# Scores and state sums of a retention layer as 64x64 quarters of TensorE, with the order of all steps rewritten

## The chip, the cores and the metric

One NeuronCore of a Trainium2 chip runs the whole program. The metric is the device time of one execution in microseconds (us); the kernel before takes 430.01 us (median of three runs, 429.88 to 433.79). All times in this document are of that kind or come from one profiled execution of the kernel.

## The reference

A chunked linear-attention ("retention") layer is followed by a gated feed-forward layer. Cut to what matters:

```python
# q, k, v: (4 batches, 8 heads, 768 positions, 64); block = 64
for b in range(12):
    intra = (qb @ kb.T * Dmask) @ vb              # inside the block
    inter = (qb * lam_pow) @ kv_state             # from all earlier blocks
    out[b] = intra + inter
    kv_state = lam ** 64 * kv_state + (kb * rev_pow).T @ vb
x_prev = x shifted by one position                # x: heads side by side, 512 wide
xk = mu_k * x + (1 - mu_k) * x_prev;  xr = mu_r * x + (1 - mu_r) * x_prev
out = sigmoid(xr @ w_r) * (relu(xk @ w_k) ** 2 @ w_v)     # 512 -> 1024 -> 512
```

## The kernel before

**Tiling.** The 768 positions are worked on as NT = 6 blocks n of 128 positions, each of two 64-position halves (eo = 0 and 1). The eight heads are four pairs hp; the two heads of a pair (ab = 0 and 1) fill the 128 partitions. For each (n, hp) there are these steps, named by one letter, and the small letters name what VectorE (DVE), ScalarE (ACT) or GpSimd (POOL) do:

- `L` and `N` (`load_hp`, `load_qv`): DMAs on SyncE's queue (SP) that bring keys, then queries and values, into one of two buffers `in` (hp 0 and 2 share one, `in_104`; hp 1 and 3 the other, `in_105`). Block 0 comes as one DMA of four parts.
- `M` (`clear`): two memsets on POOL that put zeros beside queries and values, so that a 128-row product of one head of the pair has zeros where the other head's rows would be.
- `A` (`scores`): in blocks 1 to 5, eight fp32 matmuls, each with 128 rows (both heads), 64 output columns of the array and 128 moving columns; half of the moving operand is zeros. Result in the PSUM tile `sc`. `a` (`decay`) multiplies it by the decay mask into the SBUF tile `mv` on DVE, and `q` (`decay_queries`) puts the scaled queries beside it (four DVE instructions).
- `U` (`sums`): eight fp32 matmuls of the same shape, keys against values with zeros, into the PSUM tile `u`: the state's increments of both halves. Block 5 needs only the first half and already used 64x64. `u` and `w` (`even_state`, `odd_state`) update the state on DVE and copy it beside the values on ACT.
- `B` (`values`): sixteen fp32 matmuls of 128 rows, 64 array columns and 64 moving columns, into the PSUM tile `xp`.
- `e E f F` mix the result with its shifted copy (ACT, POOL, DVE); `y x` split it into a high and a low part (ACT, DVE).

In block 0, `A`, `U` and `B` use other shapes. Then come the dense products of the feed-forward layer, each fp32 product made of three fp32r passes (high x high, high x low, low x high) of 128x128 by 512 columns: `R` and `Q` (`rp`), `K` (`kp`, with `h` and `p` on ACT and DVE after them), `V` (`vp`, with `o` multiplying by the gate and sending the output). Block 0 runs `R` and `K` as plain fp32. At the start the weights are loaded (`S`) and brought from their int64 transport form into fp32 parts (`c` on ACT and POOL, `C` on DVE, `D` on ACT and DVE).

**Order.** A string `ORDER` lists every step, such as `A21` (scores, block 2, pair 1). A loop emits them in that order, and the class `InOrder` keeps every engine's instructions in the order of emission, so that an engine whose next instruction waits does nothing else. There is no other scheduler. Because the helper class records every operation, all instructions have line L30 in the profile.

**PSUM.** Of eight banks, `sc` has two buffers of one bank, `u` and `xp` one each, and the dense products share four.

Of the kernel before, what the change touches and what calls it, by code (L numbers as in the profile page):

```python
# [7 lines left out]
F32 = mybir.dt.float32  # L8
# [25 lines left out]
def tile_retention_moe(  # L34
# [35 lines left out]
    ps_s = ctx.enter_context(tc.tile_pool(name="ps_s", bufs=2, space=bass.MemoryType.PSUM))  # L70
# [10 lines left out]
    IN = [const.tile([128, 6, 512], F32, name=f"in{i}") for i in range(2)]  # L81
    Q = [t[:, 0:5:4].rearrange("p x (b e i) -> p x b e i", b=B, e=2) for t in IN]
    VS = [t[:, 1:6:4].rearrange("p x (b a e) -> p x b a e", b=B, a=2) for t in IN]
    KT = [t[:, 2].rearrange("p (b e r) -> p b e r", b=B, e=2) for t in IN]
    KN = [t[:, 3].rearrange("p (b a d) -> p b a d", b=B, a=2) for t in IN]
# [7 lines left out]
    def load_hp(n, hp):  # L93
        t = IN[hp % 2]
        if n == 0:
            sync.dma_start(t[:, 0:4].rearrange("p c o -> p (c o)"), qvk0[hp])
            return
        sync.dma_start(t[:, 2:4].rearrange("p c o -> p (c o)"), kk[n - 1, hp])

    def load_qv(n, hp):  # L100
        t = IN[hp % 2]
        for i in range(2):
            rows, cols = slice(i * 64, i * 64 + 64), slice(i * 4, i * 4 + 2)
            sync.dma_start(t[rows, cols].rearrange("p c o -> p (c o)"), qv[n - 1, hp, rows])

    def clear(n, hp):
        t = IN[hp % 2]
        gpsimd.memset(t[64:128, 0 if n == 1 and hp < 2 else 1:2], 0.0)  # L110
        gpsimd.memset(t[0:64, 4 if n == 1 and hp < 2 else 5:6], 0.0)

# [132 lines left out]
    def scores(n, hp):  # L249
        q = Q[hp % 2]  # L250
        if n == 0:
            kt = KT[hp % 2].rearrange("p b e r -> p b (e r)")
            scs[n, hp] = [ps_s.tile([128, B, 128], F32, tag="sc", name="sc") for _ in range(2)]
            for b in range(B):
                for ab in range(2):
                    rows = slice(ab * 64, ab * 64 + 64)
                    tensor.matmul(scs[n, hp][ab][:, b], kt[rows, b], q[rows, 0, b].rearrange("p e i -> p (e i)"), start=True, stop=True)
            return
        kt = KT[hp % 2]
        scs[n, hp] = sc = ps_s.tile([128, B, 2, 64], F32, tag="sc", name="sc")  # L260
        for b in range(B):
            for eo in range(2):
                tensor.matmul(sc[eo * 64:eo * 64 + 64, b], kt[:, b, eo, :], q[:, :, b, eo, :],
                              start=True, stop=True)
# [6 lines left out]
    def decay(n, hp):  # L271
        sc, mv = scs.pop((n, hp)), mv_of(n, hp)
        if n == 0:
            mv = mvs[n, hp] = mv.rearrange("p e b a i -> p (e b a i)").rearrange("p (a b i) -> p a b i", a=2, b=B)
            for ab in range(2):
                h = 2 * hp + ab
                vector.tensor_tensor(mv[:, ab], sc[ab], Dt[:, h:h + 1].broadcast_to([128, B, 128]), op=ALU.mult)
            return
        for eo in range(2):
            rows = slice(eo * 64, eo * 64 + 64)  # L280

            i = slice(64 - eo * 64, 128 - eo * 64)
            vector.tensor_tensor(
                mv[rows, eo], sc[rows],
                Dt[rows, 2 * hp:2 * hp + 2, i].rearrange("p (o a) i -> p o a i", o=1).broadcast_to([64, B, 2, 64]),
                op=ALU.mult)

    def decay_queries(n, hp):
        q, mv = Q[hp % 2], mv_of(n, hp)
        for eo in range(2):  # L290
            dr = slice(64, 128) if eo == 0 else slice(0, 64)
            for ab in range(2):
                rows = slice(ab * 64, ab * 64 + 64)
                lp = LP[rows, 2 * hp + ab:2 * hp + ab + 1, :].broadcast_to([64, B, 64])
                vector.tensor_tensor(mv[dr, eo, :, ab, :], q[rows, ab, :, eo, :], lp, op=ALU.mult)
# [7 lines left out]
    def sums(n, hp):  # L303
        kn, vs = KN[hp % 2], VS[hp % 2]
        us[n, hp] = u = ps_1.tile([128, B, 2, 64], F32, tag="u", name="u")
        for b in range(B):
            for ab in range(2):
                if n == 0:
                    tensor.matmul(u[ab * 64:ab * 64 + 64, b, 0], kn[:, b, ab, :], vs[:, 0, b, ab, :],
                                  start=True, stop=True)  # L310
                elif n + 1 < NT:
                    tensor.matmul(u[ab * 64:ab * 64 + 64, b], kn[:, b, ab, :], vs[:, :, b, ab, :],
                                  start=True, stop=True)
                else:
                    tensor.matmul(u[ab * 64:ab * 64 + 64, b, 0], kn[0:64, b, ab, :], vs[0:64, 0, b, ab, :],
                                  start=True, stop=True)


    def to_values(n, hp, eo, x):
        for ab in range(2):  # L320
            scalar.copy(VS[hp % 2][64 - eo * 64:128 - eo * 64, eo, :, ab, :], x[ab * 64:ab * 64 + 64])


    def even_state(n, hp):
        u, state = us[n, hp][:, :, 0, :], ST[hp]
# [7 lines left out]
    def odd_state(n, hp):  # L333
        vector.scalar_tensor_tensor(ST[hp], ST[hp], LC[:, hp:hp + 1], us.pop((n, hp))[:, :, 1, :],
                                    op0=ALU.mult, op1=ALU.add)

    def values(n, hp):
        mv, vs = mvs.pop((n, hp)), VS[hp % 2]

        pool, tag = (ps_m, "m") if (n, hp) == (0, 1) else (ps_1, "xp")  # L340
        xp = pool.tile([128, B, 2, 64], F32, tag=tag, name="xp")
        for eo in range(1 if n == 0 else 2):
            for b in range(B):
                for ab in range(2):
                    rows = slice(ab * 64, ab * 64 + 64)
                    if n == 0:
                        tensor.matmul(xp[rows, b].rearrange("p e i -> p (e i)"), vs[:, 0, b, ab, :], mv[:, ab, b, :], start=True, stop=True)
                    else:
                        tensor.matmul(xp[rows, b, eo, :], vs[:, eo, b, ab, :], mv[:, eo, b, ab, :],
# [98 lines left out]
    def v_out(n, b):  # L448
# [4 lines left out]
        L=load_hp, N=load_qv, M=clear, A=scores, a=decay, q=decay_queries, k=decay_keys, U=sums, u=even_state, w=odd_state, B=values,  # L453
# [30 lines left out]
Sr0 cr0 Cr0 Z10 T0 L00 Sr1 Z1 A00 k00 U00 a00 Z2 B00 cr1 L01 u00 Cr1 Sr2 k01 A01 a01 E00 U01 cr2 L02 u01 e00 T1 B01  # L484
Sr3 E01 L03 T2 F00 k02 Cr2 A02 f00 R00 e01 cr3 a02 U02 B02 M10 k03 u02 F01 f01 A03 Cr3 U03 Sk0 e02 R01 E02 a03 ck0 N10
L10 L11 Q00 f02 F02 R02 u03 Sk1 k10 q10 B03 N11 M11 Ck0 U10 E03 A10 Sk2 F03 Q01 R03 Q02 L12 e03 f03 ck1 u10 a10 B10
Sk3 N12 w10 Sv0 Sv1 M12 k11 U11 A11 s00 Ck1 Q03 s01 q11 E10 e10 ck2 k12 f10 u11 s02 K00 h00 a11 F10 A12 B11 M13 w11
L13 E11 Ck2 e11 a12 ck3 U12 K01 u12 f11 N13 K02 k13 s03 F11 Ck3 K03 w12 x10 cv0 A13 q12 B12 h01 h02 p00 h03 E12 N20
Sv2 Cv0 cv1 a13 L20 Dv0 U13 K04 u13 K05 Cv1 q13 K06 h04 p01 Dv1 K07 Sv3 M20 cv2 w13 A20 k20 U20 V00 h05 y10 L21 Cv2
k21 F12 e12 f12 V02 B13 h06 cv3 Dv2 M21 u20 Cv3 p02 N21 w20 h07 Dv3 p03 y11 x11 Dr0 V04 V06 q20 Dr1 U21 A21 V01 E13  # L490
V03 e13 V05 V07 o00 o01 a20 F13 f13 Dk0 B20 o02 o03 L22 y13 x12 R10 Q10 R11 Q11 R12 Q12 N22 u21 a21 x13 y12 Dk1 R13
Q13 L23 s10 q22 K10 s11 M22 E20 q21 K11 e20 s12 s13 w21 f20 F20 k22 U22 h10 A22 x20 Dk2 B21 K12 M23 a22 Dk3 K13 K14
h11 e21 N23 E21 F21 K15 h12 K16 p10 f21 h13 k23 u22 w22 B22 h14 U23 x21 A23 K17 p11 h15 E22 F22 u23 w23 V10 h16 y20
L30 p12 V12 a23 k30 V14 y21 e22 f22 M30 q23 h17 x22 L31 N30 A30 U30 p13 k31 B23 L32 V16 E23 V11 e23 a30 F23 u30 q30
N31 w30 V13 f23 M31 U31 y22 o10 B30 e30 u31 o11 A31 y23 k32 V15 o12 V17 R20 o13 E30 N32 q32 f30 x23 Q20 R21 Q21 R22
Q22 R23 L33 k33 Q23 q31 a31 M32 s20 w31 F30 s21 x30 B31 E31 e31 U32 F31 u32 w32 A32 a32 f31 M33 K20 s22 h20 L40 N33
K21 s23 B32 E32 F32 A33 x32 U33 h21 K22 u33 N40 q33 h22 L41 K23 h23 p20 k41 p21 K24 K25 h24 K26 K27 a33 h25 V20 k40
h26 p22 h27 y30 p23 w33 e32 f32 x31 V22 y31 V21 M40 B33 U40 A40 L42 M41 q40 e33 E33 f33 V24 u40 F33 N41 a40 w40 y32
V23 y33 B40 A41 o20 E40 U41 a41 F40 u41 V26 e40 L43 V25 V27 q41 x33 k42 o21 w41 o22 M42 f40 N42 A42 o23 B41 N43 U42
M43 L50 E41 a42 k43 u42 R30 F41 q42 w42 Q30 R31 Q31 R32 Q32 e41 R33 f41 Q33 x40 B42 s30 s31 U43 x41 A43 a43 E42 F42  # L500
q43 s32 s33 u43 w43 K30 N50 q50 x42 h30 K31 K32 h31 p30 K33 K34 h32 h33 p31 K35 h34 K36 h35 K37 L51 V30 h36 y40 e42
k50 y41 V32 V34 f42 h37 p33 p32 U50 B43 E43 A50 u50 V31 V33 y42 e43 N51 k51 F43 o30 f43 a50 q51 V35 V36 A51 U51 o31
B50 e50 a51 f50 o32 V37 E50 o33 u51 R40 Q40 F50 R41 Q41 B51 R42 Q42 x50 L52 k52 L53 x43 E51 F51 R43 y43 Q43 s40 N52
U52 N53 u52 q52 A53 s41 a53 s42 A52 K40 h40 q53 K41 h41 a52 s43 k53 K42 K43 h42 p40 K44 K45 K46 h43 h44 x51 p41 h45
e51 h46 f51 p42 K47 B52 h47 U53 y50 u53 p43 y51 V40 V42 e52 V41 E52 f52 V43 V44 F52 o40 y52 V46 V45 V47 B53 o41 o42
o43 x52 e53 f53 y53 R50 Q50 R51 Q51 R52 Q52 E53 F53 x53 R53 Q53 s50 s51 K50 K51 s52 h50 s53 h51 K52 h52 K53 h53 p51
p50 K54 h54 K55 h55 K56 K57 h56 h57 p53 V50 V52 V54 p52 V51 V53 o50 o51 V56 V55 V57 o52 o53
# [54 lines left out]
```

## Time and profile before

| | |
|---|---|
| time, three runs | 430.01 us median (429.88 to 433.79) |
| span of the profiled execution | 430.3 us |
| PE (matmuls) busy | 419.5 us |
| DVE busy | 264.0 us |
| ACT busy | 204.9 us |
| POOL busy | 71.0 us |
| HBM read, written | 35.83 MB, 6.29 MB |

The span is the profiled execution's own time: it lies 0.3 us above the median of the runs. An execution of a matmul is shown as one record for each of its passes: an fp32 matmul leaves two, so that the eight matmuls of `A` are 16 records, and the sixteen of `B` are 32. `sc<-in` reads: the tile `sc` is written from the tile `in`; `128*64 128x128` reads: 128 rows by 64 columns of the array, moving operand 128 partitions by 128 columns. Matmuls are pipelined and their shown ends are modelled, so that the distance of two starts, not a duration, is what one costs in a stream.

### The profile page before, as it was taken

The numbers are of one execution on the slowest core, as the hardware profiler recorded it, in microseconds if no ns is written. First come the engines' busy times: TensorE is split into PE (matmuls) and PEld (weight loads), VectorE is DVE, ScalarE is ACT, GpSimd is POOL, SyncE is SP. The second block draws the span as 40 slices with busy tenths as digits, with TensorE's granted clock in tenths as the row PEclk, the third lists the DMA queues.
The fourth block names the chain that finished last, engine by engine and source line by source line (L and its number), as shares of the span: only waits on it lengthen the run. The fifth ranks groups of instructions, "written<-read, shape, count | busy, mean of one in ns | idle before, by whom it ended". The sixth has DMA issues, their size and how long they took to land.

```text
span 430.3 us, 7314 instructions
## 1 busy us (share of the span) xinstructions
PE 419.5 (98%) x2935; PEld 328.9 (76%) x2935; DVE 264.0 (61%) x402; ACT 204.9 (48%) x357; POOL 71.0 (16%) x142
## 2 busy tenths in 40 slices
PE   7998899999999999999999999999999999999996
PEld 4665545668888888888888888888878888888885
DVE  5886999979867674746667646555437561414411
ACT  3645686586677643344644434454244460224300
POOL 4366554331102011110020200000000000000000
PEclk9999999999999999999999999999999999999999
DMA  7889918131403213515004523004520001100001
GB/s 295 304 308 330 300 48 277 66 97 50 146 3 99 87 46 107 153 58 140 0 2 131 187 78 99 0 0 123 161 62 0 2 1 50 50 2 0 0 30 69
DMA packets 12306, 42.60 MB, mean 99 GB/s; under 512 B 1776, under 2 KB 2160, under 8 KB 10736
## 3 DMA queue, kind: packets, MB, share of 16 engines
q1 hardware_dynamic: 8672, 35.84, 26.5%
q10 hardware_dynamic: 3600, 6.29, 4.0%
q8 instruction: 23, 0.38, 0.4%
q14 instruction: 11, 0.09, 0.1%
HBM read 35.83 MB, written 6.29 MB: 98 GB/s over the span
## 4 chain that ended last, share of the span: by engine, by line
PE 81%; DVE 7%; DMA 6%; ACT 2%; POOL 1%; issue 1%; SPq 0%; DVEq 0%; ACTq 0%
PE vp L30 29%; PE kp L30 26%; PE rp L30 13%; PE xp L30 5%; PE sc L30 4%; DMA wst<-w_k 4%; PE u L30 3%; DMA in<-qv 2%; DVE wst L30 2%; DVE mv L30 1%; DVE lov L30 1%; PE table L30 1%; ACT wu L30 1%; DVE wu L30 1%; POOL wu L30 1%
## 5 line engine op out<-in xcount | busy, mean ns | idle before, releaser
L30 PE MATMUL vp<-hiv,k 128*128 128x512 f32 (+1 forms) x400 | 122.8, 384 | 1.0 <-ACT kf L30 1.0
L30 PEld LDWEIGHTS vp<-hiv,k 128*128 128x128 f32 x400 | 74.1, 188 | 16.9 <-ACT kf L30 1.4
L30 PE MATMUL vp<-lov,k 128*128 128x512 f32 (+1 forms) x200 | 76.2, 381 | 0.0
L30 PE MATMUL kp<-xh,hik 128*128 128x512 f32 x160 | 62.9, 393 | 0.0
L30 PE MATMUL kp<-xl,hik 128*128 128x512 f32 x160 | 62.3, 389 | 0.0
L30 PE MATMUL kp<-xh,lok 128*128 128x512 f32 x160 | 62.3, 389 | 0.0
L30 ACT ACTIVATE ts<-xp,omu 128x512 f32<-128x512 f32 x48 | 31.8, 684 | 62.5 <-PE xp L30 44.2
L30 DVE TENSOR_TENSOR kf<-kp,kf 128x512 f32<-128x512 f32 x40 | 27.4, 688 | 37.2 <-ACT kf L30 37.1
L30 ACT ACTIVATE kf<-kp 128x512 f32<-128x512 f32 x48 | 28.4, 594 | 37.6 <-PE kp L30 37.2
L30 ACT COPY in<-st 64x256 f32<-64x256 f32 x80 | 32.3, 404 | 22.1 <-DVE st L30 17.8
L30 PEld LDWEIGHTS vp<-lov,k 128*128 128x128 f32 x200 | 37.6, 188 | 6.9
L30 DVE TENSOR_TENSOR mv<-sc,Dt 64x512 f32<-64x512 f32 (+1 forms) x48 | 32.6, 686 | 12.3 <-PE sc L30 11.9
L30 DVE TENSOR_TENSOR xl<-ts,xh 128x512 fp32r<-128x512 f32 x40 | 27.7, 703 | 19.3 <-ACT xh L30 19.2
L30 DVE SCALAR_TENSOR_TENSOR ts<-xp,smalls,ts 128x512 f32<-128x512 f32 x40 | 29.6, 747 | 15.8 <-ACT ts L30 15.6
L30 DVE TENSOR_TENSOR mv<-in,LP 64x256 f32<-64x256 f32 x80 | 34.5, 431 | 3.2 <-DMA in<-qv 1.6
L30 DVE TENSOR_TENSOR k<-kf,k 128x1024 fp32r<-128x1024 f32 x24 | 29.1, 1223 | 10.7 <-ACT k L30 10.7
L30 DVE TENSOR_TENSOR rt<-vp,rt 128x512 f32<-128x512 f32 (+1 forms) x25 | 16.4, 665 | 31.5 <-PE vp L30 31.2
L30 PEld LDWEIGHTS kp<-xh,hik 128*128 128x128 f32 x160 | 30.0, 188 | 7.0 <-issue 0.9
L30 PEld LDWEIGHTS kp<-xh,lok 128*128 128x128 f32 x160 | 30.0, 188 | 6.3
L30 PEld LDWEIGHTS kp<-xl,hik 128*128 128x128 f32 x160 | 30.0, 188 | 6.0
L30 ACT CAST xh<-ts 128x512 fp32r<-128x512 f32 x40 | 24.1, 616 | 21.7 <-DVE rt L30 18.2
L30 DVE SCALAR_TENSOR_TENSOR st<-st,LC,u 128x256 f32<-128x256 f32 x36 | 17.2, 478 | 24.8 <-ACT in L30 20.0
(70 smaller groups left out, 586.3 us busy)
## 6 DMA issues: line engine op xcount, KB each, us to landing
in<-qv SPq DMA_DIRECT2D x40, 256.0 KB, 4.5
in<-kk SPq DMA_DIRECT2D x20, 512.0 KB, 4.6
out<-rt ACTq DMA_DIRECT2D x23, 256.0 KB, 2.0
in<-qvk SPq DMA_DIRECT2D x4, 1024.0 KB, 6.3
wst<-w_k SPq DMA_DIRECT2D x4, 1024.0 KB, 9.2
wst<-w_v SPq DMA_DIRECT2D x4, 1024.0 KB, 9.7
wst<-w_r SPq DMA_DIRECT2D x4, 512.0 KB, 7.1
out<-rt ACTq DMA_DIRECT2D x2, 128.0 KB, 1.7
```

What stands on the lines that cost most here:

```text
L30: return lambda *args, **kw: self.tc.keep_in_program_order(op(*args, **kw))
```

## The change

In blocks 1 to 5, `A` and `U` become sixteen matmuls on quarters of the array: each has 64 rows (one head in `A`, one half of the positions in `U`), 64 columns and 64 moving columns, and the sixteen go round the four quarters. The multiplications by zeros are gone, and with them the step `M` and the sixth part of the `in` buffer. The two row halves write to different PSUM banks, so each step needs two banks instead of one. Two neighbouring pairs hp share them: `sc` is one tile of two banks for a pair of pairs; the first halves of `u` go to the bank of tag `u`, the second halves to the bank of tag `xp`, for both pairs together. `B` of an even hp then uses the bank of `u`, of an odd hp that of `xp`. Block 5's `U` keeps its eight matmuls.

```diff
-    ps_s = ctx.enter_context(tc.tile_pool(name="ps_s", bufs=2, space=bass.MemoryType.PSUM))
+    ps_s = ctx.enter_context(tc.tile_pool(name="ps_s", bufs=1, space=bass.MemoryType.PSUM))
...
-    def clear(n, hp):
-        t = IN[hp % 2]
-        gpsimd.memset(t[64:128, 0 if n == 1 and hp < 2 else 1:2], 0.0)
-        gpsimd.memset(t[0:64, 4 if n == 1 and hp < 2 else 5:6], 0.0)
...
     def scores(n, hp):
...
-        kt = KT[hp % 2]
-        scs[n, hp] = sc = ps_s.tile([128, B, 2, 64], F32, tag="sc", name="sc")
+        if hp % 2 == 0:
+            pair = ps_s.tile([128, 2, 2, B, 64], F32, tag="sc", name="sc")
+            scs[n, hp], scs[n, hp + 1] = pair[:, :, 0], pair[:, :, 1]
         for b in range(B):
             for eo in range(2):
-                tensor.matmul(sc[eo * 64:eo * 64 + 64, b], kt[:, b, eo, :], q[:, :, b, eo, :],
-                              start=True, stop=True)
+                for ab in range(2):
+                    rows = slice(ab * 64, ab * 64 + 64)
+                    tensor.matmul(scs[n, hp][eo * 64:eo * 64 + 64, ab, b], kt[rows, b, eo, :], q[rows, b, eo, :],
+                                  start=True, stop=True)
...
     def sums(n, hp):
...
-                elif n + 1 < NT:
-                    tensor.matmul(u[ab * 64:ab * 64 + 64, b], kn[:, b, ab, :], vs[:, :, b, ab, :],
-                                  start=True, stop=True)
+        halves = range(2 if n + 1 < NT else 1)
+        if hp % 2 == 0:
+            for eo in halves:
+                pair = ps_1.tile([128, 2, B, 64], F32, tag=("u", "xp")[eo], name="u")
+                us[n, hp, eo], us[n, hp + 1, eo] = pair[:, 0], pair[:, 1]
...
+                for eo in halves:
+                    rows = slice(eo * 64, eo * 64 + 64)
+                    tensor.matmul(us[n, hp, eo][ab * 64:ab * 64 + 64, b], kn[rows, b, ab, :], vs[eo][rows, b, ab, :],
...
     def values(n, hp):
...
-        pool, tag = (ps_m, "m") if (n, hp) == (0, 1) else (ps_1, "xp")
+        pool, tag = (ps_m, "m") if (n, hp) == (0, 1) else (ps_1, "u" if n > 0 and hp % 2 == 0 else "xp")
...
-Sr0 cr0 Cr0 Z10 T0 L00 Sr1 Z1 A00 k00 U00 a00 Z2 B00 cr1 L01 u00 Cr1 Sr2 k01 A01 a01 E00 U01 cr2 L02 u01 e00 T1 B01
+Sr0 L00 cr0 Z10 T0 Z1 A00 k00 T2 Cr0 U00 a00 cr1 L01 Cr1 Z2 B00 u00 A01 Sr2 E00 k01 e00 L02 a01 Sr3 F00 f00 U01
...
```

All lines of `ORDER` are new. Three places show what that means for single engines.

First, TensorE's order where block 2 begins, with what each row waits for. Before, in block 2 (pairs 1 and 0 are `in_105` and `in_104`):

```order
L30 MATMUL u<-in_105 64x128 [waits DMAHW2_49,DMAHW1_49,DMAHW3_49,DVE_49,Pool_49]
L30 MATMUL u<-in_105 64x128 x7
L30 MATMUL sc<-in_105 64x128 x8
```

and with the change, `A20`, `U20`, `U21`, `A21`:

```order
L30 MATMUL sc<-in_104 64x64 [waits DMAHW7_49,DMAHW0_49]
L30 MATMUL sc<-in_104 64x64 [waits DMAHW1_49]
L30 MATMUL sc<-in_104 64x64 x14
L30 MATMUL u<-in_104 64x64 [waits PE_49] x2
L30 MATMUL u<-in_104 64x64 x14
L30 MATMUL u<-in_105 64x64 [waits DMAHW6_49,DMAHW5_49]
L30 MATMUL u<-in_105 64x64 [waits DMAHW6_49]
L30 MATMUL u<-in_105 64x64 x14
L30 MATMUL sc<-in_105 64x64 [waits DVE_49]
L30 MATMUL sc<-in_105 64x64 x15
```

The steps of two pairs now stand together, and the second pair's scores wait for VectorE, which reads the first pair's scores out of the shared banks.

Second, the start on TensorE, where block 0 begins, as a piece of the difference (`table<-lone` is the step `T2`, a table of decay powers; `sc` and `u` are `A00` and `U00`):

```order
 L30 MATMUL idle<-zeros 128x512
 L30 MATMUL sc<-in_104 128x128 x8
+L30 MATMUL table<-lone 128x512
 L30 MATMUL u<-in_104 64x64 x8
 L30 LDWEIGHTS zeros
```

`T2` has moved from behind `B01` to ahead of `U00`, and so ahead of `B00`, the last reader of the first load buffer, which follows two filler matmuls later.

Third, SP's queue at the same stage. Before:

```order
L30 DMA in_104<-qvk 128x2048
L30 DMA wst<-w_r 128x1024
L30 DMA in_105<-qvk 128x2048
L30 DMA wst<-w_k 128x2048
L30 DMA in_104<-qv 64x1024 x2
L30 DMA in_104<-kk 128x1024
L30 DMA in_105<-kk 128x1024
L30 DMA wst<-w_k 128x2048
```

and with the change:

```order
L30 DMA in_104<-qvk 128x2048
L30 DMA wst<-w_r 128x1024
L30 DMA wst<-w_k 128x2048
L30 DMA in_105<-qvk 128x2048
L30 DMA wst<-w_k 128x2048
L30 DMA in_104<-kk 128x1024
L30 DMA in_104<-qv 64x1024 x2
L30 DMA in_105<-kk 128x1024
```

The first two loads of `w_k` have moved ahead of the last load of block 0 and of the first loads of block 1.

## Prediction before the run

> **What bounds the kernel now.** I read the page first, then TensorE's waits, then single stretches of its timeline. From the page: the busy times, and TensorE (PE) and VectorE (DVE) in 40 slices.
>
> ```profile
> PE 419.5 (98%) x2935; PEld 328.9 (76%) x2935; DVE 264.0 (61%) x402; ACT 204.9 (48%) x357; POOL 71.0 (16%) x142
> PE   7998899999999999999999999999999999999996
> DVE  5886999979867674746667646555437561414411
> ```
>
> TensorE is full from the fifth slice on, while VectorE is full only between about 40 and 80 us. The waits of TensorE, all of them:
>
> ```profile
> PE idle L30 <- DVE zeros L30: 2.0, 1, 2.0
> PE sc L30 <- DMA in<-qv: 1.6, 1, 1.6
> PE xp L30 <- DVE mv L30: 1.4, 1, 1.4
> PE vp L30 <- ACT kf L30: 1.0, 1, 1.0
> PE sc L30 <- DMA in<-qvk: 0.5, 1, 0.5
> PE table L30 <- DVE rows L30: 0.3, 1, 0.3
> ```
>
> Their sum is 6.8 us, and in the timeline the last falls before 93 us. What is taken off TensorE's stream after that comes off the time; before it, DMA and VectorE must keep up too.
>
> **What a small step costs.** Timeline of TensorE, dense products and a group of steps of block 2, and a group of block 5 (start, length):
>
> ```profile
> 221.68 0.39 PE L30 MATMUL vp<-hiv,k 128*128 128x512 f32 x1
> 221.91 0.39 PE L30 MATMUL vp<-lov,k 128*128 128x512 f32 x1
> ...
> 223.81 1.15 PE L30 MATMUL xp<-mv,in 128*64 128x64 f32 x32
> 224.79 1.04 PE L30 MATMUL u<-in 128*64 128x128 f32 x16
> 225.67 1.04 PE L30 MATMUL sc<-in 128*64 128x128 f32 x16
> ...
> 304.11 1.09 PE L30 MATMUL sc<-in 128*64 128x128 f32 x16
> 305.13 0.68 PE L30 MATMUL u<-in 64*64 64x64 f32 x16
> 305.74 1.15 PE L30 MATMUL xp<-mv,in 128*64 128x64 f32 x32
> ```
>
> From start to start, `U` costs 0.88 us (224.79 to 225.67): 16 records in eight pairs of 0.110. Two records must run side by side on the two column halves, since a full-width record of 512 columns takes 0.44 (9.28 us for 21, below) and so one of 128 columns alone 0.11. `B` costs 0.98 for 32 records of 64 columns, its entry included; 0.93 elsewhere (51.20 to 52.13, below), that is 16 pairs of 0.058. Row halves run side by side too: in block 0 `A` has eight matmuls of 64 rows, and its 16 records of 128 columns take 1.09 (8.95 to 10.04), where one after another they would take 16 x 0.11 = 1.76.
>
> ```profile
> 8.95 1.16 PE L30 MATMUL sc<-in 64*128 64x128 f32 x16
> 10.04 0.92 PE L30 MATMUL u<-in 128*64 128x64 f32 x16
> 51.20 1.13 PE L30 MATMUL xp<-mv,in 128*64 128x64 f32 x32
> 52.13 1.07 PE L30 MATMUL u<-in 128*64 128x128 f32 x16
> 53.13 9.28 PE L30 MATMUL kp<-x,wk 128*128 128x512 f32 x21
> ```
>
> **The change part by part.**
>
> *Quarters.* A changed `A` or `U` has 16 matmuls, 32 records of 64 columns, like `B`. With four quarters at work it is eight rounds of 0.058 = 0.47 us instead of 0.88, a gain of 0.41. There are 20 `A` (blocks 1 to 5) and 16 `U` (blocks 1 to 4): 36 x 0.41 = 14.8 us. No row shows four at once. The upper bound for a step is that of `B`, two at a time: 0.93, and the 36 steps would lose 1.9. I take 0.47: row halves and column halves each overlap fully in the rows above. The Trainium skill, "TensorE: Matmul & The Clock Gate", section "Measured speedup vs the span model", says that row and column packing compose; no run here shows it yet.
>
> *Changes of tile shape.* Block 5's `U` (0.61, 305.13 to 305.74) has 16 records in eight pairs of 0.058, 0.47, and so 0.14 for the change from 128*64 to 64*64; the `sc` ahead of it costs 1.02 instead of 0.88 in the same way. There are five such changes inside groups of block 5; in the new order block 5's groups hold `A` and `U` alone or `B` alone. That takes away 5 x 0.14 = 0.7. I count 25 stretches of small steps between dense products in both orders, so the entries and exits stay as many.
>
> *The early waits.* Rows of the timelines of SP, TensorE and ACT before 100 us:
>
> ```profile
> 12.73 0.33 SPq L30 DMA_DIRECT2D in<-qvk  x1
> 17.26 1.13 PE L30 MATMUL table<-lone 128*128 128x512 f32 x2
> 36.73 1.15 ACT L30 ACTIVATE wu<-wst 128x1024 f32<-128x1024 f32 x1 [1.44 <-DMA wst<-w_k]
> 39.99 1.41 PE L30 MATMUL xp<-mv,in 128*64 128x64 f32 x32 [1.35 <-DVE mv L30]
> 40.70 1.20 SPq L30 DMA_DIRECT2D in<-qv  x2
> 50.30 1.09 PE L30 MATMUL sc<-in 128*64 128x128 f32 x16 [1.59 <-DMA in<-qv]
> 93.04 0.50 PE L30 MATMUL vp<-hiv,k 128*128 128x512 f32 x1 [0.99 <-ACT kf L30]
> ```
>
> The first wait (39.99) comes from ACT, which stood at a `w_k` that SP had queued behind loads of block 1 (36.73), with the state's copies and so `a10` behind it. The second follows from the first: its `qv` could be issued only when that `B10` was done with the buffer (40.70). The new queue has two loads of `w_k` ahead of block 1. The third is the conversion of `w_v`. All three should go: -4.0. `T2` now stands ahead of `B00`, costs 1.1 there, and moves the third `qvk` load (12.73), which waits for `B00`, and so the start of the dense work: +1.1 (0 if the DMA engines are the limit, 2 if the last `qvk` load, now behind a `w_k`, comes later still).
>
> *VectorE while it converts weights.* By windows of 20 us:
>
> ```profile
> 40.00:60.00 20.00, 18.37 (x156) 10.90 (x157) 18.91 (x26) 14.54 (x29) 12.11 (x15) 1.00 0.79 249
> 60.00:80.00 20.00, 20.00 (x105) 9.99 (x103) 19.51 (x24) 16.59 (x26) 10.58 (x7) 1.00 0.54 184
> 80.00:100.00 20.00, 19.01 (x155) 15.02 (x154) 16.40 (x20) 12.35 (x19) 6.32 (x7) 1.00 0.20 54
> ```
>
> The third busy number is VectorE's: 38.4 of 40 us. If TensorE gets there earlier, VectorE must too. The new order has 105 VectorE instructions up to the last low part of `w_v`, the old one 116, and the eleven that now stand behind it are `q`, state updates and splits of 0.4 to 0.7 us, about 5 us of work. TensorE comes some 6 us earlier there (8 steps x 0.41 and 4.0 less 1.1). I take the difference and less, +0.7, from 0 to 4.
>
> *New waits.* `A21` waits for `a20`, in the shared banks (first piece of order shown), `A23` for `a22` and `U31` for `u30` likewise. VectorE's prices:
>
> ```profile
> L30 DVE TENSOR_TENSOR mv<-sc,Dt 64x512 f32<-64x512 f32 x40 | 27.4, 686 | 9.8 <-PE sc L30 9.4
> L30 DVE SCALAR_TENSOR_TENSOR st<-st,LC,u 128x256 f32<-128x256 f32 x36 | 17.2, 478 | 24.8 <-ACT in L30 20.0 <-PE u L30 4.2
> L30 DVE TENSOR_TENSOR mv<-in,LP 64x256 f32<-64x256 f32 x80 | 34.5, 431 | 3.2 <-DMA in<-qv 1.6
> ```
>
> `a20` takes 2 x 0.69 = 1.4 after `A20` and some 0.2 to be seen; TensorE has `U20` and `U21` in between, 0.94. So 0.7 is left, and behind it `K10` waits as everything on TensorE does. `A23`: the same, with more queued ahead on VectorE, 1.0. `U31`: `u30` 0.48 and two crossings, with nothing on TensorE in between, 0.8. Sum +2.5; none if VectorE were instant, up to 9 if it is 2 us behind each time (four `q` of 0.43 ahead). The other groups have both `A` ahead of both `a`, and from block 2 on there are 42 or more dense matmuls ahead of `B`, 0.23 us apart (221.68 to 221.91), 9.7 us, against 4.6 us of VectorE work for the `a`, `u` and `w` of two pairs; these I cost at nothing, and they would cost what VectorE is late.
>
> *POOL's memsets* cost nothing: POOL is busy 16%, and what waits for them is not on the path. *The end*: `o52` was behind the last half of the last output on VectorE; now the last half is last, alone.
>
> ```profile
> 426.30 1.02 DVE L30 TENSOR_TENSOR rt<-vp,rt 128x256 f32<-128x256 f32 x2 [5.19 <-PE vp L30]
> out<-rt ACTq DMA_DIRECT2D x23, 256.0 KB, 2.0
> out<-rt ACTq DMA_DIRECT2D x2, 128.0 KB, 1.7
> ```
>
> VectorE's tail goes from 1.0 to 0.4, and the last transfer from 256 to 128 KB saves some 0.1 to 0.3: -0.7.
>
> **Sum** against the profiled 430.3: -14.8 -0.7 -4.0 +1.1 +0.7 +2.5 -0.7 = 414.4. The median of the runs lies 0.3 below the span: 414 us.
>
> **Rivals.**
>
> 1. *Not four at once.* Something other than the columns sets the pace, such as a fixed time for each start; `B` starts 32 records in 0.93, 29 ns each. Then a step is 0.93 and the sum is 414.4 + 36 x 0.46 = 431, no change. For it: no row has four. Against: a window of 20 ns at the beginning of block 5's `U` holds two starts.
>
> ```profile
> 305.12:305.14 0.02, 0.01 (x2) 0.01 (x2) 0.00 (x0) 0.00 (x0) 1.00 0.00 0
> ```
>
> The Trainium skill, "TensorE: Matmul & The Clock Gate", section "Wait — 56ns, not 53.3ns?", gives about 25 ns from start to start however small a matmul; by that 32 starts are an estimated 0.80 and the time would be 426, and the trace disagrees with two starts in 20 ns. 10%.
>
> 2. *Three rounds for two.* The two passes of a matmul keep the other pair of quarters waiting, so that four matmuls take about 0.145 instead of 0.116: 0.58 a step, 36 x 0.11 = 4.0 more, 418. 12%.
>
> 3. *The new waits bite.* VectorE is late in the conversion (+3) or in most of the nine half-blocks' handovers through two banks (0.5 each): 418 to 423, say 420. For it: 38.4 of 40 us busy, and one buffer less. Against: after 120 us VectorE is busy 162.5 of 310 us.
>
> ```profile
> 120.00:430.30 310.30, 306.26 (x2110) 254.46 (x2108) 162.54 (x254) 128.74 (x231) 20.01 (x73) 1.00 0.20 60
> ```
>
> 15%.
>
> 4. *Slower: the quarters run one after another.* If row halves overlap only at full width and column halves only at full height, 32 records of 0.058 make 1.86 a step: 414.4 + 36 x 1.39 = 464. It turns slower from the point where a step costs more than 1.03 (430.3 x 1.01 less 414.4, over 36, on top of 0.47). Against it: block 5's `U` uses the 64*64 shape, and its two quarters overlap. 5%.
>
> **How the numbers follow.** Forecast 58%, 409 to 418 by its own bounds (waits gone and VectorE in time, or half of the upper bounds); rival 2 12%, rival 3 15%, rival 1 10%, rival 4 5%. The range 409 to 424 leaves out rivals 1 and 4 and little else. A measurement of this kernel tells about 1% from no change. Faster by over 1% (below 425.7): 58 + 12 + 15 and a little of rival 1 = 85%; within 1%: 10%; slower: 5%.
>
> **What would show it.** In the changed profile a 64*64 `sc` of 32 records should be followed by its neighbour after 0.47 us; 0.58, 0.93 or 1.86 would show rivals 2, 1 or 4. TensorE's waits should list `sc` on DVE `mv` and `u` on DVE `st` with some 2.5 us together, and no `vp` on ACT `kf` at 90 us. TensorE should be busy about 404 us. If TensorE's waits sum to over 10 us, rival 3 holds.

## The result and the profile after

The changed kernel takes 416.36 us in the median of four runs (415.41 to 416.75), the kernel before, beside it, 430.37 (429.88 to 433.79): a ratio of 0.9648, with a 95% interval of 0.9614 to 0.9681. Forecast were 414.0 us, 409 to 424. The profiled execution has a span of 413.6 us and a time of 415.41. (In the diff shown above, the first new line of `ORDER` lacks one token: `Sr1` stands between `k00` and `T2`.)

From the page of the changed kernel, the busy times and VectorE's share in 40 slices:

```profile
PE 404.0 (98%) x3511; PEld 315.5 (76%) x3511; DVE 261.2 (63%) x402; ACT 204.4 (49%) x357; POOL 53.4 (13%) x110
DVE  6789888988776776746747565656745663345002
```

TensorE has 576 more records than before and 15.5 us less busy time (419.5); 404 was forecast. The time came off TensorE's own stream; it is still the engine that is full. VectorE has two slices at 9 where it had five.

The waits of TensorE, all that are listed (in total, times, longest):

```profile
PE idle L30 <- DVE zeros L30: 2.0, 1, 2.0
PE sc L30 <- DVE mv L30: 1.2, 2, 0.6
PE vp L30 <- DVE lov L30: 0.9, 1, 0.9
PE table L30 <- DVE rows L30: 0.8, 1, 0.8
PE u L30 <- DVE st L30: 0.7, 1, 0.7
PE sc L30 <- DMA in<-qvk: 0.5, 1, 0.5
PE rp L30 <- DVE x L30: 0.3, 1, 0.3
```

The waits on `qv`, on the first `mv` and on `kf` are gone. `sc` on `mv` (twice) and `u` on `st` are the new waits in the shared banks, 1.9 us together as listed here. `vp` on `lov`, the low half of the value weights, is new as well.

TensorE's timeline, at the low half of the weights, at block 2 and at block 4:

```profile
76.64 0.50 PE L30 MATMUL vp<-lov,k 128*128 128x512 f32 x1 [0.95 <-DVE lov L30]
...
110.53 0.69 PE L30 MATMUL sc<-in 64*64 64x64 f32 x32
111.05 1.11 PE L30 MATMUL u<-in 64*64 64x64 f32 x64
112.74 0.69 PE L30 MATMUL sc<-in 64*64 64x64 f32 x32 [0.58 <-DVE mv L30]
...
264.43 0.39 PE L30 MATMUL rp<-hir,xl 128*128 128x512 f32 x1
264.74 0.69 PE L30 MATMUL sc<-in 64*64 64x64 f32 x32
265.26 1.11 PE L30 MATMUL u<-in 64*64 64x64 f32 x64
266.19 0.65 PE L30 MATMUL sc<-in 64*64 64x64 f32 x32
266.77 0.50 PE L30 MATMUL vp<-hiv,k 128*128 128x512 f32 x1
```

Read starts, not durations. The two `u` steps take 266.19 - 265.26 = 0.93 us for 64 records: 0.465 a step, 14.5 ns from start to start on the average. The whole group of four steps, from the first `sc` to the next dense matmul, takes 266.77 - 264.74 = 2.03.

### The profile page after: what moved, and what is told of

Read it like the earlier page. It is cut to its first block, busy times and chain, and to the rows that moved or that the text cites. A ratio compares the mean times of both kernels' runs of the same rounds, so it can differ in the third digit from the quotient of the medians.

```text
span 413.6 us, 8367 instructions
## 1 busy us (share of the span) xinstructions
PE 404.0 (98%) x3511; PEld 315.5 (76%) x3511; DVE 261.2 (63%) x402; ACT 204.4 (49%) x357; POOL 53.4 (13%) x110
## 4 chain that ended last, share of the span: by engine, by line
PE 88%; DVE 4%; DMA 3%; POOL 2%; ACT 1%; issue 0%; SPq 0%; DVEq 0%; ACTq 0%
PE vp L30 32%; PE kp L30 28%; PE rp L30 16%; PE xp L30 5%; PE sc L30 3%; POOL wu L30 2%; PE u L30 2%; DMA wst<-w_r 2%; DMA in<-qv 1%; DVE wst L30 1%; DVE mv L30 1%; ACT wu L30 1%; PE table L30 1%; DMA rows<-hot 1%; DVE rows L30 1%; DVE wu L30 1%
## 5 line engine op out<-in xcount | busy, mean ns | idle before, releaser
L30 PEld LDWEIGHTS vp<-hiv,k 128*128 128x128 f32 x400 | 74.1, 188 | 14.9
L30 DVE TENSOR_TENSOR kf<-kp,kf 128x512 f32<-128x512 f32 x40 | 26.8, 688 | 36.5 <-ACT kf L30 36.4
L30 POOL COPY lastw<-ts 128x4 f32<-128x4 f32 x40 | 11.4, 284 | 184.0 <-ACT ts L30 183.7
```

Source lines behind the costliest of these rows:

```text
L30: return lambda *args, **kw: self.tc.keep_in_program_order(op(*args, **kw))
```

## The experiments

All but the last were made from the changed kernel. Where several rounds were run, the ratio is to the kernel before on the same chip.

| run | time, us | ratio (95%) | span of the profile, us |
|---|---|---|---|
| changed kernel, first yardstick | 415.17 | 0.9643 (0.9627 to 0.9659) | 413.4 |
| changed kernel, second yardstick, beside the first `no_waits` | 416.40 | 0.9662 (0.9622 to 0.9701) | 414.4 |
| rowhalf | 420.78, one run | | 419.0 |
| onequarter | 441.95, one run | | 440.2 |
| pairs | 416.88, one run | | 415.1 |
| no_bank_wait | 415.55 | 0.9658 (0.9629 to 0.9687) | 413.4 |
| no_waits | 414.46 | 0.9583 (0.9543 to 0.9622) | 412.6 |
| no_waits, again | 412.07 | 0.9564 (0.9523 to 0.9604) | 409.5 |
| late_weights | 413.05 | 0.9572 (0.9530 to 0.9613) | 411.6 |
| t2_back | 415.96 | 0.9651 (0.9606 to 0.9696) | 413.8 |
| memsets | four runs, 416.51 to 422.77 | 0.9728 (0.9664 to 0.9792) | 414.7 |
| kernel before, for its profile | 430.65 | 0.9994 (0.9955 to 1.0032) | 428.1 |

### The yardsticks

> The changed kernel once more, on the chip of the other runs of this call, as their yardstick: 415.4 to 416.8 us, its span some 1.8 us below its time.

> The changed kernel as the yardstick of this call: 415.2 us, span 413.4.

The first came out 0.2 us under the range expected, the second 1.2 us above what was expected. In every execution here the time lies 1.7 to 1.9 us above the span (415.17 and 413.4 of the changed kernel, 430.67 and 428.9 of that before). One kernel's executions scatter by some us: those of the second yardstick have spans of 414.1 to 417.7.

### Do four quarters work at once, and does the order matter?

The theory is that a step costs eight rounds because all four quarters stream together. The rival is that something else sets 0.465 us. Three orders of the same sixteen matmuls tell.

`rowhalf`, only column halves alternate (the same in `sums`):

```diff
-        for b in range(B):
-            for eo in range(2):
-                for ab in range(2):
+        for ab in range(2):
+            for b in range(B):
+                for eo in range(2):
```

> The loops over the four quarters are turned round so that the row half is the outermost: of matmuls that follow each other only the column half alternates, while all work is the same. Forecast's theory (a quarter starts when it is free, but matmuls start in program order): two quarters work at a time, a step of 32 rises from 0.47 to about 0.93 us, 36 steps add 16.6 us, span about 430. Rival (the engine finds a free quarter whatever the order, or the time of a step is set by something else than the four quarters, such as a fixed time for each start): the steps stay at 0.47 and the span at 413.6.

`onequarter`, four matmuls that follow each other use the same quarter:

```diff
-        for b in range(B):
-            for eo in range(2):
-                for ab in range(2):
+        for eo in range(2):
+            for ab in range(2):
+                for b in range(B):
```

> The loop over the four blocks of one quarter is the innermost: four matmuls that follow each other use the same quarter. Forecast's theory: they run one after another but for the last of a quarter, which can overlap the first of the next; a step of 32 rises from 0.47 to between 1.5 and 1.86 us, 36 steps add 37 to 50 us, span 451 to 464. Rival (order does not matter): 413.6.

Measured were spans of 419.0 and 440.2. Neither number was in either expectation: order matters, but less than a start in program order would make it. TensorE's timeline of `onequarter`, the group of block 4 that was shown of the changed kernel:

```profile
284.91 1.36 PE L30 MATMUL sc<-in 64*64 64x64 f32 x29
286.06 0.27 PE L30 MATMUL u<-in 64*64 64x64 f32 x1
286.11 0.22 PE L30 MATMUL sc<-in 64*64 64x64 f32 x1
...
286.17 0.22 PE L30 MATMUL sc<-in 64*64 64x64 f32 x1
...
286.23 0.22 PE L30 MATMUL sc<-in 64*64 64x64 f32 x1
286.28 2.29 PE L30 MATMUL u<-in 64*64 64x64 f32 x58
288.36 0.27 PE L30 MATMUL sc<-in 64*64 64x64 f32 x1
...
289.82 0.50 PE L30 MATMUL vp<-hiv,k 128*128 128x512 f32 x1
```

All `sc` of this step stand ahead of all `u` in the program. Yet the first `u` starts at 286.06, when three of the 32 `sc` records have still to start, and the two kinds then take turns (single `u` start at 286.16 and 286.22). So a quarter has a short line of its own: the start goes on to the next quarter when the last three records of this one are lined up. A turn of one quarter, eight records, takes 0.29 us (eight turns from 286.06 to 288.36). One record that streams and three that wait would make it four rounds of 0.058, 0.23; where the other 0.05 goes is not shown. A step is 286.06 - 284.91 = 1.15 us, not 1.86, and the group of four 4.91 instead of 2.03. For 36 steps that is 2.88 / 4 x 36 = 25.9 us; the span rose by 25.8 to 26.8. The same group in `rowhalf`:

```profile
268.56 0.80 PE L30 MATMUL sc<-in 64*64 64x64 f32 x26
...
271.23 0.50 PE L30 MATMUL vp<-hiv,k 128*128 128x512 f32 x1
```

2.67 us, 0.64 more, for 36 steps 5.8; the span rose by 4.6 to 5.6. (After 26 `sc` the first `u` start, with six to come: three in each of two quarters.)

The line of three was read from these runs, so it was put to a test that could fail. `pairs` lets two matmuls in a row use the same quarter, which is four records: one that streams and three that wait.

```diff
-        for b in range(B):
-            for eo in range(2):
-                for ab in range(2):
+        for eo, ab, two in [(eo, ab, two) for two in (0, 2) for eo in range(2) for ab in range(2)]:
+            for b in (two, two + 1):
```

> In scores and state sums two matmuls that follow each other use the same quarter, then two the next quarter, all else as in the changed kernel. The runs with the row half outermost (419.0) and with one quarter at a time (440.2) fitted neither a start in strict program order (430 and 451 to 464) nor a free choice of quarter (413.6): there the next quarter started when three records of the one before were still to start. Theory (each quarter has a short line of its own, of about three records, and the start goes on to the next quarter as soon as the last fits into it): four records in a row fit, one streaming and three waiting, all four quarters stay busy, the step stays at 0.47 and the span at 413 to 415. Rival (starts in program order): the second matmul of each two waits for the first, 8 times 0.117 us a step, 0.93, span about 430.

```profile
265.79 0.73 PE L30 MATMUL sc<-in 64*64 64x64 f32 x30
...
267.96 0.50 PE L30 MATMUL vp<-hiv,k 128*128 128x512 f32 x1
```

The group takes 2.17, 0.14 more than with the quarters in turn, and the span is 415.1, 0.1 above the range expected, where starts in program order would give 430. A line of about three holds. With it, 0.465 us as the pace of four busy quarters is shown: the same sixteen matmuls cost more, 0.50, 0.63 and 1.15 us a step, the longer the order keeps them on one quarter or one pair of quarters. (0.50 and 0.63 are 0.465 and a quarter of the 0.14 and 0.64 that the group of four steps took more.)

The Trainium skill, "TensorE: Matmul & The Clock Gate", section "The mechanism", says that matmuls start and end strictly in program order. The rows disagree: three `sc` records start after a `u` that stands behind them in the program.

### What the new waits are worth

`no_bank_wait` puts VectorE's reader of the first step (`a20`) behind the second step (`A21`), which so has nothing of VectorE's left to wait for; likewise at `A23` and `U31`.

```diff
-f12 x13 Dk0 Q11 Q12 R12 R13 Q13 q20 y13 A20 N21 U20 y12 s10 s13 a20 s11 U21 s12 A21 L23 K10 Dk2 a21 u21 q21 K12 h10
+f12 x13 Dk0 Q11 Q12 R12 R13 Q13 q20 y13 A20 N21 U20 y12 s10 s13 s11 U21 s12 A21
+a20 L23 K10 Dk2 a21 u21 q21 K12 h10
...
-... N23 a22 p12 p13 U23 A23 y20 ...
+... N23 U23 A23 a22 p12 p13 y20 ...
...
-... U30 y22 u30 U31 K22
+... U30 y22 U31 u30 K22
```

> The three places where the first small matmuls of a pair follow those of the other pair into the same banks get a piece of work of TensorE between them (k convolution pieces or state outputs that stood just behind), so that VectorE has read the banks by then. Theory (these three waits are time of the path): the waits of 0.65, 0.65 and 0.72 us go, 2.0 us less than the changed kernel. Rival (the wait only moves to the next thing that VectorE owes TensorE): less than 0.7 us.

(The expectation misnames the edit: no work of TensorE is put between; VectorE's reader is moved behind.) The profile's waits of TensorE, the three largest behind the opening one:

```profile
PE table L30 <- DVE rows L30: 1.3, 1, 1.3
PE vp L30 <- DVE lov L30: 1.0, 1, 1.0
PE sc L30 <- DMA in<-qvk: 1.0, 1, 1.0
```

The bank waits are gone, and yet the median is that of the changed kernel, 415.55 to 415.17. The opening of this execution was slow, as a row of its timeline and the same row of the first yardstick show (the scores of the third pair of block 0):

```profile
21.41 1.16 PE L30 MATMUL sc<-in 64*128 64x128 f32 x16 [1.00 <-DMA in<-qvk]
```

```profile
18.66 1.16 PE L30 MATMUL sc<-in 64*128 64x128 f32 x16 [0.35 <-DMA in<-qvk]
```

From there to the end it is 413.4 - 21.41 = 392.0 us, against 394.7: 2.7 less. The waits did leave the stream, and the opening took as much back. The stretch that holds the three waits and not the opening, from the first scores of block 2 to those of the group of block 4, shows what they are worth. In `no_bank_wait`:

```profile
112.80 0.69 PE L30 MATMUL sc<-in 64*64 64x64 f32 x32
...
114.25 0.65 PE L30 MATMUL sc<-in 64*64 64x64 f32 x32
...
264.49 0.69 PE L30 MATMUL sc<-in 64*64 64x64 f32 x32
```

That is 151.7 us, and 264.74 - 110.53 = 154.2 in the changed kernel: 2.5. The two yardsticks, `t2_back` and `memsets`, which keep the waits, have 154.2 to 154.3; the three versions below, which have none, 151.7. It is more than the 1.9 listed, because a listed wait begins at the shown end of the matmul before it, and that end is modelled. From start to start, `A21` comes 112.74 - 111.05 = 1.69 us after the `u` steps, where it comes 0.94 after them without the wait.

The medians did not show the gain, so a second edit moves the second of the four splits of the value weights (`Dv1`) ahead of a key decay. There VectorE had run short:

```profile
70.79 0.70 DVE L30 TENSOR_SCALAR wu<-wu 128x1024 int32<-128x1024 int32 x1 [1.34 <-POOL wu L30]
...
74.53 3.19 DVE L30 TENSOR_TENSOR lov<-wst,hiv 128x1024 fp32r<-128x1024 f32 x2
```

(the changed kernel's VectorE: 1.34 us without work, then 3.7 us of other steps, and behind them the `lov` for which TensorE waits at 76.64).

```diff
-k12 h04 f11 Cv2 y10 h07 U12 Dv1 U13 cv3 Dv2 ...
+Dv1 k12 h04 f11 Cv2 y10 h07 U12 U13 cv3 Dv2 ...
```

> The three bank waits taken away as before (work of VectorE's readers moved behind the second small step), and the first weight conversion of the values moved ahead of a key decay, so that VectorE does not run short there (the wait on the low half of the weights at 76.6 us, 0.95 to 1.2). Theory (each wait of TensorE on the chain of the end is worth its length, and only the opening, which waits for the first transfers, hid it in the earlier run, where the first scores of the third pair came at 21.4 instead of 18.7 us): from the eighth dense record on, 3.0 us less than the changed kernel, and 2 to 3 us less in the median, 412.4 to 413.2. Rival (the waits only move on): less than 1 us.

Its median is 1.9 us under the second yardstick, just under the 2 to 3 expected. Its profile has a new wait, in the opening of block 1. TensorE, then ACT, then ACT of the yardstick:

```profile
40.43 0.69 PE L30 MATMUL u<-in 64*64 64x64 f32 x32 [1.75 <-ACT st L30]
```

```profile
38.25 0.91 ACT L30 ACTIVATE in<-in,KD 128x256 f32<-128x256 f32 x2 [4.52 <-DMA in<-kk]
```

```profile
34.68 0.91 ACT L30 ACTIVATE in<-in,KD 128x256 f32<-128x256 f32 x2 [0.78 <-DMA in<-kk]
```

The keys of block 1's second pair came 3.6 us later, and ACT, which keeps its order, with them. So it was run once more.

> The kernel with the three bank waits and the wait on the low half of the weights taken away, once more, beside the next one: 410.0 to 413.2 in span, in two heaps (410.0 and 412.6) by whether the keys and values of the second pair of block 1 land in time.

TensorE's largest wait behind the opening one (2.0 on `zeros`) is now:

```profile
PE rp L30 <- DVE x L30: 0.6, 1, 0.6
```

All four waits are gone and none has come in their place; only the one on `x` is 0.3 longer. The span is 409.5, 3.9 under the first yardstick's 413.4: 1.3 up to the first scores of block 2 (108.91 against 110.23), where the wait on `lov` stood, and 2.6 from there to the group of block 4 (260.60 against 264.49), where the bank waits stood. The six spans, 409.5 to 411.3 and one of 413.1, do not fall into the two heaps expected. Both medians, 414.46 and 412.07, are under those of the changed kernel. This version beats both kernels: 0.9564 and 0.9583 of the time before, against 0.9643 to 0.9662.

To take the late keys away too, `late_weights` issues a 1 MB load of the keys' weights behind the queries and values of that pair.

```diff
-... k10 q10 Sk2 Q02 k11 s00 N11 Sk3 Sv0 s01 ...
+... k10 q10 Q02 k11 s00 N11 Sk2 Sk3 Sv0 s01 ...
```

> The same kernel with one weight load of SyncE (the second last of the keys' weights, 1 MB) issued behind the queries and values of block 1's second pair rather than ahead of them. Theory (those 0.5 MB share the transfer engines with 1 MB that is needed later, and land up to 11 us after their issue): the wait of 1.75 us on the second pair's state does not come, all executions lie near 410 in span, the median 411.8 to 412.3. Rival (the keys are late for another reason, or the weights are then late in turn): the median stays at 414 or rises.

The ratio is that of `no_waits`, the median, 413.05, lies between what theory and rival say, and the profiled span is 411.6. The wait on the state does not show, but neither did it in the second `no_waits`. The theory is not borne out: what makes these transfers late in some executions stays open.

### Two edits forecast to cost something, or nothing

`t2_back` puts `T2` back behind `B01`.

```diff
-Sr0 L00 cr0 Z10 T0 Z1 A00 k00 Sr1 T2 Cr0 U00 ...
-cr2 T1 B01 Cr2 ...
+Sr0 L00 cr0 Z10 T0 Z1 A00 k00 Sr1 Cr0 U00 ...
+cr2 T1 B01 T2 Cr2 ...
```

> The third opening table step (16 small table matmuls, 2.0 us of TensorE) moved back to where the kernel before had it, behind the first values of the second pair. Forecast's theory (it stands ahead of the first values and delays them by 1.1 us): 0.4 to 1.1 us less. Rival (the opening waits for the third transfer of queries, values and keys, whatever TensorE does before): within 0.4 us, and TensorE's wait for that transfer grows by about what the step took.

(The expectation misnames the step: `T2` is the two `table<-lone` matmuls, 1.1 us.) The changed kernel, then `t2_back`, TensorE and SP's queue:

```profile
10.24 1.12 PE L30 MATMUL table<-lone 128*128 128x512 f32 x2
13.63 0.33 SPq L30 DMA_DIRECT2D in<-qvk  x1
...
19.26 1.16 PE L30 MATMUL sc<-in 64*128 64x128 f32 x16 [0.51 <-DMA in<-qvk]
```

```profile
12.67 0.33 SPq L30 DMA_DIRECT2D in<-qvk  x1
17.72 1.13 PE L30 MATMUL table<-lone 128*128 128x512 f32 x2
18.90 1.16 PE L30 MATMUL sc<-in 64*128 64x128 f32 x16
```

The span is 413.8 and the ratio 0.9651: nothing. With `T2` at 10.24 the third `qvk` load is issued 1.0 us later, and TensorE waits for it ahead of the third scores; with `T2` at 17.72 there is no such wait, and `T2` itself stands ahead of them. Its 1.1 us lie ahead of the third scores in both orders. These start at 18.90 in the one, at 18.66, 19.26 and 19.64 in three executions of the other. The rival's "within 0.4 us" came true. Its remark on the wait did not: the wait does not grow, it is filled. Whether the transfer would decide without `T2` is not shown.

`memsets` puts GpSimd's clearing back, on a buffer that nobody reads (40 calls; the kernel before had 32).

```diff
         xps[n, hp] = xp.rearrange("p b e i -> p b (e i)")
+        if n + 1 < NT:
+            gpsimd.memset(spare[64:128], 0.0)
+            gpsimd.memset(spare[0:64], 0.0)
```

> Two GpSimd memsets of 64x512 on a spare buffer are put back in each step of values of blocks 0 to 4, as the kernel before had them, 40 in all. Theory (GpSimd stands off the path, its share is 13%): time unchanged within 0.3 us. Rival (they cost VectorE or GpSimd's own conversions time, in the stretch where these are late): 1 us or more, and the wait on the low half of the weights grows.

The profile's span is 414.7 against 414.4 and the wait on `lov` 1.5 against 1.3: as the theory said. But its ratio, 0.9728, lies 0.0066 above the yardstick's, and the two intervals overlap. The run does not settle it.

### The kernel before, a second profile

> The kernel before once more, for its profile. Spans of its executions so far: 428.2 to 429.2 in most, 431.0 to 432.1 in others, 430.3 in the one that the forecast was made from. Theory (that execution held waits for transfers that most executions do not: the 1.6 us of the third pair's scores on the queries and values at 50.3, or the 1.35 at 40.0): in an execution of 428.2 to 429.2 the sum of these two waits is smaller by 1 to 2 us, and all else reads alike. Rival (the difference is spread over the whole, for instance in TensorE's pace): both waits are there, and the eleven hundred steady matmuls are shorter.

Its two largest waits of TensorE behind the opening one (2.0 on `zeros`; no other is over 0.3), and two rows of its timeline, which answer to those at 39.99 and 50.30 in the prediction:

```profile
PE vp L30 <- ACT kf L30: 1.1, 1, 1.1
PE xp L30 <- DVE ts L30: 0.5, 1, 0.5
```

```profile
38.90 1.15 PE L30 MATMUL xp<-mv,in 128*64 128x64 f32 x32
...
47.29 1.09 PE L30 MATMUL sc<-in 128*64 128x128 f32 x16
```

The theory holds: with a span of 428.1, neither of the two waits is there, and 0.5 us on `ts` has come instead. 1.35 + 1.59 - 0.5 = 2.4 us, and the spans differ by 2.2. These two waits belong to an execution, not to the kernel.

## Why the prediction was right, point by point

| term | forecast, us | measured, us |
|---|---|---|
| quarters, 36 steps | -14.8 | -14.9 (0.88 less 0.465, by 36) |
| tile shapes in block 5 | -0.7 | the changes are gone |
| early waits | -4.0 | all gone; -1.6 against the second profile of before |
| `T2` ahead of `B00` | +1.1 | 0 |
| VectorE in the conversion | +0.7 | +0.95 (`vp` on `lov`; 1.2 in the yardstick) |
| new waits | +2.5 | +2.5 (1.9 as listed) |
| POOL's memsets | 0 | 0.3 in profiles, not settled |
| tail | -0.7 | -0.95 |

*Quarters.* Right in mechanism and size. The inference from row halves and column halves, each seen to overlap in the profile before, held for both together. Rivals 1, 2 and 4, with 0.93, 0.58 and 1.86 a step, are refuted by the starts: 0.465, and `rowhalf` and `onequarter` show what quarters without work cost. (Rival 2's numbers do not fit its name: three rounds for two would be 0.70 a step and some 423, not 0.58 and 418. Neither came.) Whole stretches say the same: from the first small start to the next dense one, those of blocks 2 to 5 sum to 44.8 us in the profile before and to 32.3 in the second `no_waits`, which has no wait in them. That is 12.5 less, where 28 steps at 0.41 and the 0.7 for tile shapes make 12.2. No run puts the quarters into the old order or the new order without the quarters, so these sums, not a run, part the two.

The Trainium skill's floor of about 25 ns from start to start ("TensorE: Matmul & The Clock Gate", section "Wait — 56ns, not 53.3ns?") would have made a step of 32 records an estimated 0.80; the trace has 14.5 ns on the average.

*Tile shapes.* A group of block 5, two `A` and two `U`, now takes 331.50 - 329.48 = 2.02 us, what the group of block 4 takes; nothing is left for a change of shape inside it.

```profile
329.48 0.69 PE L30 MATMUL sc<-in 64*64 64x64 f32 x32
...
331.50 0.50 PE L30 MATMUL vp<-hiv,k 128*128 128x512 f32 x1
```

*Early waits.* All three are gone, but two of them for another reason than was given. The prediction put those at 39.99 and 50.30 down to a `w_k` queued behind loads of block 1. A second execution of the kernel before, with the same queue, has neither. So 2.9 of the 4.0 are no work of the change, and that the new queue would prevent such waits is not shown: in the first `no_waits` late keys still cost 1.75. The third, on `kf`, is in both profiles of before (1.0 and 1.1) and is gone; the wait on `lov`, about as long, has come in the same `vp` products of block 0.

*New waits.* The mechanism was right at all three places, and so was the sum: from start to start `A21` comes 0.75 later than without a wait (0.7 was worked out), `A23` as much (1.0, for work queued ahead of it on VectorE that did not delay it), and `U31` 0.84 (0.8). Rival 3 did not come: TensorE's waits sum to 6.4, not to 10.

*VectorE.* Late by about what was said, but not by being overloaded. It had stood idle 1.34 us for GpSimd some 4 us before, and the order of a few steps decided it: in `no_waits` VectorE has the same work, and the wait is gone.

*`T2`.* Wrong. The step that failed is that it "moves the third `qvk` load [...] and so the start of the dense work: +1.1". The load did go out later, at 13.63 against 12.73. But the kernel before also had `T2` ahead of the dense work, at 17.26, right ahead of the third scores at 18.90. Taking it away there gained what it cost at its new place, and the sum left that out. The bound of 0 came true; its condition, that the DMA engines are the limit, is not shown.

*The tail.* The last output row of VectorE started 4.0 us before the end (426.30 of 430.3) and now starts 3.0 before it:

```profile
410.57 0.42 DVE L30 TENSOR_TENSOR rt<-vp,rt 128x256 f32<-128x256 f32 x1 [2.18 <-PE vp L30]
```

*From span to time.* The sum, 414.4, was within 1 us of the span, 413.6. The failed step is the next one, "the median of the runs lies 0.3 below the span". It set the span of one execution, which held 2.4 us more of waits than the other profile of the same kernel, against the median of others. In one and the same execution the time lies 1.8 above the span, and 414.4 + 1.8 = 416.2 stands beside a median of 416.36. These waits did no harm to the sum, since what was in the base was also taken off; they did to the difference, which is 14.0 us in the medians and 16.7 in the two first profiles.

That the sum came within 1 us is in part luck, since its errors cancel. With what was measured it is 430.3 - 14.8 - 0.7 - 0.3 (the rest of the 12.5 above) - 4.0 + 0.95 + 2.5 - 0.95 = 413.0, and two small waits, on `rows` (0.8 instead of 0.3) and on `x` (0.3, new), make it 413.8. From the span of the second profile of before, 428.1, to that of the first yardstick it is -14.8 -0.7 -0.3 -1.6 +1.2 +2.5 +0.3 -0.95 = -14.35, so 413.75, and the yardstick has 413.4.

## What to carry to other kernels

Where matmuls use a quarter of the array, let those that follow each other go round all four quarters: here 32 records then took 0.465 us, and 1.15 when four matmuls in a row used one quarter. A wait that is in one profile need not be in the next: before a wait for a transfer in the opening is counted as a gain, look at a second execution, and hold a time against the span of the same execution. Here the waits for shared banks were worth their length from start to start, 2.5 us, and not the 1.9 of the list, and letting the second writer go ahead of the first reader took them away.

## What the runs showed of the hardware

Two things. First, how close starts come. A window of 30 ns at the beginning of the group of block 4 in the changed kernel (busy time and number of records):

```profile
264.74:264.77 0.03, 0.03 (x5) 1.00 0.00 0
```

One of the five is the dense matmul of 264.43, whose shown end lies in the window; the other four are the first `sc`, all started within 30 ns; records on one quarter start 0.06 apart (286.11, 286.17, 286.23 above), so these four are on four quarters. Second, records overtake others that stand ahead of them in the program, when those wait for a busy quarter, by about three records for each quarter (the `u` at 286.06). What it costs when both row halves write to the same bank was not tried.
